# A fused adaLN transformer block, forward and backward: LN1, modulation and the first K, Q, V by chunks of 512 tokens between the first attention units, and db1 stored as a row

## The chip, the cores and the metric

The kernel runs on one core of one Trainium2 chip. The metric is the device time of one execution in microseconds (us), lower is better. Each result is the median of several executions on one chip, taken beside executions of the kernel before on the same chip.

## The reference

One block with 2048 tokens, width 512, 32 heads of 16, MLP width 1792, in bfloat16, and all its gradients from `grad_out`:

```python
mod = silu(c) @ w_mod                      # sa, ca, ga, sb, cb, gb: six rows of 512
h   = layernorm(x) * (1 + ca) + sa         # LN1 and modulation
x   = x + ga * (softmax_attention(h @ wqkv) @ wo)
h   = layernorm(x) * (1 + cb) + sb
x   = x + gb * (relu(h @ w1 + b1)**2 @ w2 + b2)
# outputs: x, dx, dwqkv, dwo, dw1, db1, dw2, db2, dc, dw_mod
```

## The kernel before

The forward attention runs over 64 units: four blocks of 512 queries, eight groups of four heads, two head pairs. Each unit has 16 steps of 128 keys: scores on TensorE, one exponential of 128x1024 on ScalarE, P·V on TensorE two steps later. "Background" generators give TensorE other work between the steps: in the first query block the K and Q of the other head groups, later the MLP. TensorE's order is the program's; the order on the other engines is a scheduler's.

Before the first unit the kernel does everything for LN1 at once (cuts marked `...`):

```python
# opening: modulation as full rows, then columns out of them
nc.sync.dma_start(wmod[:], io["w_mod"]...)                      # 3 MB
for (n0, nw) in chunks(6 * D, 512): ...                         # 24 matmuls 128x512
...
nc.scalar.activation(rstd[:], mv[:, :, 1], ACT.Sqrt, ...)       # LN1, all 16 token tiles
for st in range(ST):
    nc.scalar.activation(xhat_tm[:, st, :], x_tm[:, st, :], ACT.Identity, bias=nmr..., scale=rstd...)
...                                                             # all transposes, 1+ca into the weights
for t in range(2):
    for s0 in range(0, S, 512):
        for _ in self.gen_fm(ps, t, 0, s0, ...): pass           # K and Q of head group 0
...
load_q(0, 0, 0)                                                 # both back from DRAM
KT = load_k(0)
```

One block of K or Q, with its evicted copy (`ev_fm`) and its transposed copy for the backward pass (`ev_tm`):

```python
def gen_fm(self, ps, t, g, s0, eng="vector"):
    ...                                                          # 4 matmuls into PSUM
    nc.vector.tensor_scalar(ev[:], pt[:], bc, None, ALU.add)     # ev_fm
    nc.sync.dma_start((self.QTq_d, self.KTq_d)[t][g, :, s0:s0 + 512], ev[:])
    nc.sync.dma_start_transpose(tm[:]..., ev[:])                 # ev_tm
    nc.gpsimd.tensor_copy(tmc[:], tm[:, :, :, 0:DH])
    nc.gpsimd.dma_start((self.qtm_d, self.ktm_d)[t][g, ...], tmc[:]...)
```

At the end of each unit VectorE normalises the output:

```python
accbank = accp.tile([P, 2, 2, 4, DH + 1], F32, name="accbank")
...
acc = accbank[:, n % 2]
...
nc.vector.reciprocal(self.rl[...], acc[:, a, :, DH])
nc.vector.tensor_tensor(O32[...], acc[:, a, :, 0:DH], ..., ALU.mult)
```

At the transition from forward to backward:

```python
nc.gpsimd.memset(t[:], 0.0)                                      # eight masked K/V tiles, 128x2048
...
db1_b = w1p.tile([P, FT], BF16, name="db1_b", bufs=1)
nc.gpsimd.dma_start(io["out_5"].rearrange("(t p) -> p t", p=P), db1_b[:])   # db1 as a column
```

The softmax here doesn't subtract the row's maximum and nothing guards it: scores larger than these inputs give would overflow.

## Time and profile before

3033.77 us, median of three executions (3030.78 to 3035.01). The profiled one spans 3026.2 us. On the page, engines' busy time is given in tenths for 40 equal slices of some 76 us; this is ScalarE's row in the profile of before:

```profile
ACT  3489999999999974217777777777777777777443
```

A 9 means that ScalarE is busy for 90% or more of the slice, as in the forward attention; the first slices and slices 15 to 18 are where it starves. Counting exponentials in ScalarE's timeline gives stage borders, good to some 0.3 us:

| border, start in us | before |
|---|---|
| first exponential | 110.5 |
| first of the third unit (33rd) | 144.7 |
| first of the second query block (257th) | 369.4 |
| last of the forward pass | 1115.8 |
| first of the backward pass | 1348.2 |
| last of the backward pass | 2836.3 |
| span | 3026.2 |

A query block has 256 exponentials at a pitch of 0.925 us, which is 236.8 us; what it takes beyond that is stalls.

### The profile page before, as it was taken

What the parts mean: (1) busy time and instruction counts of PE and PEld (TensorE: products, weight loads), DVE (VectorE), ACT (ScalarE), POOL (GpSimd) and SP (SyncE); (2) the same over time, 40 slices, a digit from 0 to 9 for tenths busy, and PEclk for the clock granted to TensorE, in tenths of its full rate; (3) what the DMA queues carried; (4) which work ended last, traced back from release to release, by engine and by line L of the source; (5) the groups of instructions that cost most, each with busy time, mean ns of one, the idle gap of its engine ahead of it and who ended that gap; (6) DMA issues with size and microseconds to landing.
All of it is one profiled execution on the core that took longest, in us unless ns stands there. A gap on an engine that the chain in (4) does not pass through costs nothing. (4 is left out here: it accounts for less than half of the span.)

```text
span 3026.2 us, 72535 instructions
## 1 busy us (share of the span) xinstructions
PE 2726.1 (90%) x29894; PEld 1416.7 (47%) x30394; DVE 1797.7 (59%) x2804; ACT 2257.3 (75%) x3378; POOL 364.2 (12%) x616
## 2 busy tenths in 40 slices
PE   3689889999999997799999999999999999999796
PEld 1345545555555543644444444444444444444343
DVE  4422123322322343458878888888888888888575
ACT  3489999999999974217777777777777777777443
POOL 2343111320221132440000000000000000000000
PEclk7899999999999999899999999999999999999898
DMA  3974231530441347969999999999999999999941
GB/s 125 220 176 119 68 83 49 123 89 26 111 108 41 91 128 143 225 140 191 191 202 189 197 203 188 208 189 197 199 189 207 190 200 195 188 191 182 225 134 61
DMA packets 1305071, 467.71 MB, mean 155 GB/s; under 512 B 1237090, under 2 KB 1268836, under 8 KB 1304740
## 3 DMA queue, kind: packets, MB, share of 16 engines
q1 hardware_dynamic: 1275972, 376.78, 66.1%
q0 software_dynamic: 28240, 84.70, 10.1%
q8 instruction: 237, 3.88, 0.5%
q10 hardware_dynamic: 528, 1.57, 0.1%
q14 instruction: 94, 0.77, 0.1%
HBM read 85.99 MB, written 67.11 MB: 51 GB/s over the span
## 5 line engine op out<-in xcount | busy, mean ns | idle before, releaser
L1190 ACT ACTIVATE pu<-st 128x512 bf16<-128x512 f32 x2048 | 1133.3, 598 | 358.1 <-PE st L1188 302.3
L1195 DVE TENSOR_TENSOR ds<-dp,pu 128x1024 bf16<-128x1024 f32 x1024 | 1208.8, 1220 | 237.6 <-ACT pu L1190 229.7
L359 ACT ACTIVATE pu<-st 128x1024 bf16<-128x1024 f32 x1024 | 955.2, 1050 | 51.1 <-PE st L356 46.3
L1188 PE MATMUL st<-KTm,QTq 128*128 128x512 bf16 x2048 | 779.4, 381 | 12.2 <-ACT pu L1190 11.5
L1138 PEld LDWEIGHTS <-dsT 128*128 128x128 bf16 x8192 | 487.6, 96 | 493.9 <-DMA dsT<-ds 21.5
L1191 PE MATMUL dp<-VTm,dOTq 128*128 128x512 bf16 x1779 | 673.7, 379 | 7.2 <-DVE ds L1195 5.9
L356 PE MATMUL st<-QTm,KTq 128*128 128x512 bf16 x1937 | 591.1, 382 | 55.5 <-issue 17.6
L1138 PE MATMUL accq<-Kg,dsT 128*128 128x16 bf16 x8192 | 493.7, 170 | 30.8 <-DMA dsT<-ds 16.1
L326 PEld LDWEIGHTS <-pu 128*128 128x128 bf16 x8192 | 354.5, 96 | 297.0 <-issue 63.9
L326 PE MATMUL accbank<-Vaug,pu 128*128 128x17 bf16 x8192 | 358.5, 171 | 43.2 <-DVE O L334 35.0
L1118 PE MATMUL acckv<-ds,Qg 128*16 128x512 bf16 x2048 | 308.6, 381 | 0.9 <-DVE ds L1195 0.7
L1118 PE MATMUL acckv<-pu,dOg 128*16 128x512 bf16 x2048 | 308.6, 381 | 0.0
L1188 PEld LDWEIGHTS <-QTq 128*128 128x128 bf16 x2048 | 196.0, 96 | 219.6 <-issue 214.8
L356 PEld LDWEIGHTS <-KTq 128*128 128x128 bf16 x2048 | 194.2, 96 | 210.8 <-issue 164.6
L1191 PEld LDWEIGHTS <-dOTq 128*128 128x128 bf16 x2048 | 197.4, 96 | 37.9 <-DVE ds L1195 16.2
L1046 POOL DMA_DIRECT2D wqkv<-in_A_wqkv_dram x1 | 0.8, 791 | 1498.3 <-DMA dsT<-ds 1498.3
L462 DVE TENSOR_SCALAR ev_fm<-pps,bcol 128x512 bf16<-128x512 f32 x60 | 45.0, 751 | 145.4 <-PE pps L454 78.7
L333 DVE RECIPROCAL rl<-accbank 128x4 f32<-128x4 f32 x128 | 23.0, 180 | 179.0 <-PE accbank L326 178.9
L309 POOL DMA_DIRECT2D QTm<-QTq_d x128 | 65.1, 512 | 439.0 <-PE st L356 395.3
L916 DVE TENSOR_SCALAR rT<-pps,bias 128x512 bf16<-128x512 f32 x42 | 31.5, 751 | 116.1 <-PE pps L913 116.0
L924 DVE SCALAR_TENSOR_TENSOR auT<-pps,rT 128x512 bf16<-128x512 f32 x42 | 29.1, 692 | 86.1 <-PE pps L922 71.0
L454 PE MATMUL pps<-xhat1T,wpad 128*128 128x512 bf16 x223 | 78.5, 391 | 0.3 <-issue 0.2
(311 smaller groups left out, 2097.1 us busy)
## 6 DMA issues: line engine op xcount, KB each, us to landing
KTq<-KTq_d POOLq DMA_DIRECT2D x32, 512.0 KB, 3.8
duT_d<-auT POOLq DMA_DIRECT2D x4, 1792.0 KB, 8.2
aT_d<-rT POOLq DMA_DIRECT2D x4, 1792.0 KB, 12.8
QTq_d<-ev_fm SPq DMA_DIRECT2D x32, 128.0 KB, 2.4
QTm<-QTq_d POOLq DMA_DIRECT2D x128, 32.0 KB, 2.1
KTq_d<-ev_fm SPq DMA_DIRECT2D x32, 128.0 KB, 2.0
VTq_d<-vT POOLq DMA_DIRECT2D x4, 1024.0 KB, 6.2
O_d<-O POOLq DMA_DIRECT2D x4, 1024.0 KB, 6.2
```

What stands on the lines that cost most here:

```text
L309: nc.gpsimd.dma_start(QTm[j][32 * j:32 * j + 32, :], self.QTq_d[g, 32 * j:32 * j + 32, 512 * qc:512 * (qc + 1)])
L326: nc.tensor.matmul(acc[:, a, sub, :], lhsT=pu[:, a, sub * P:(sub + 1) * P], rhs=Vaug[:, kb, h, :], start=(kb == 0 and a == 0 and sub == 0) ...
L356: nc.tensor.matmul(stt[:, a, :], lhsT=KT[:, kb * P:(kb + 1) * P], rhs=QTm[2 * jp + a][:], start=True, stop=True)
L359: nc.scalar.activation(pu[:], stt[:], ACT.Exp, scale=self.scale)
L454: nc.tensor.matmul(pt[:], lhsT=self.wpads[t][:, kt, g, :], rhs=self.xhat1T[:, kt, s0:s0 + 512], start=(kt == 0), stop=(kt == DT - 1))
L462: nc.vector.tensor_scalar(ev[:], pt[:], bc, None, ALU.add)
L1118: nc.tensor.matmul(acckv[r:r + DH, :], lhsT=T[n][:, ib, col:col + DH], rhs=src[:, a, :], start=(ib == 0), stop=(ib == ST - 1))
L1138: nc.tensor.matmul(accq[:, ib, a, :], lhsT=dsT[:, (i * 2 + a) * 4 + sub, :], rhs=T["K"][:, 4 * c + sub, col:col + DH], start=(c == 0 and i ...
L1188: nc.tensor.matmul(stt[:], lhsT=T["QT"][:, q], rhs=masked["KT"][2 * jp + a][:, c0:c0 + 512], start=True, stop=True)
L1190: nc.scalar.activation(pu[:, a, :], stt[:], ACT.Exp, scale=self.scale)
L1191: nc.tensor.matmul(dp[:, a, :], lhsT=T["dOT"][:, q], rhs=masked["VT"][2 * jp + a][:, c0:c0 + 512], start=True, stop=True)
L1195: nc.vector.tensor_tensor(dsg[:, i], dp[:], pu[:], ALU.mult)
```

## The change

The intent: exponentials should start before LN1 is done for all tokens, and the K tile should not go through DRAM first. A generator does 512 tokens at a time: two chunks before the first scores, the third and fourth before key blocks 4 and 8 of the first unit. (1+ca) and sa are applied where the transposes are evicted, from modulation columns that come from one-column matmuls. Other parts: the masked memsets go to VectorE, db1 leaves as a row, O32 of the last block is loaded at once on SyncE, and the transposes of `wo` and `w2` come later.

```diff
-        load_q(0, 0, 0)
-        KT = load_k(0)
+        KT = kp.tile([P, S], BF16, name="KTq")
         with tc.manual_schedule(engines={mybir.EngineType.PE}):
+            first = self.gen_open(Vaug, KT, QTm, stp)
+            next(first)
 ...
                     if kb == ST // 2 and n + 1 < len(order):
+                        if n < 2 * NQ - 1 and jp == 1:
+                            bg.until(g + 1)
 ...
+                    if n == 0 and kb % 4 == 0:
+                        next(first, None)
 ... in gen_open, for each chunk of four token tiles:
+            nc.vector.tensor_scalar(ve[:, b], mv[:, b, 1], EPS, None, ALU.add)
+            nc.gpsimd.tensor_tensor(self.rstd1[:, b], ve[:, b], self.mhalf[:], ALU.pow)
+            nc.vector.scalar_tensor_tensor(nmr[:, b], ...)
 ...                                    xhat: odd tiles on GpSimd, even ones on ScalarE
+            tp = stp.tile([P, DT, 512], BF16, name="st")
+            for kt in range(DT):
+                for k in range(4):
+                    nc.tensor.transpose(tp[:, kt, k * P:(k + 1) * P], xhat1[...], self.ident[:])
+                if kt % 2:
+                    nc.vector.tensor_scalar(dst, tp[:, kt, :], self.opcaT[...], self.mod_col(0)[...], ...)
+                else:
+                    nc.scalar.activation(dst, tp[:, kt, :], ACT.Identity, bias=..., scale=...)
 ...                                    K of group 0 straight into KT, then V
-                nc.gpsimd.memset(t[:], 0.0)
+                nc.vector.memset(t[:], 0.0)
 ...
-            nc.gpsimd.dma_start(io["out_5"].rearrange("(t p) -> p t", p=P), db1_b[:])
+            nc.scalar.copy(db1_row[:, ft * P:(ft + 1) * P], csb_ps[0:1, :P])
+        nc.gpsimd.dma_start(io["out_5"].rearrange("(o f) -> o f", o=1), db1_row[:])
```

## The prediction

> **What bounds the kernel now.** One core, 3033.77 us. The page comes first: the forward attention holds ScalarE (1024 exponentials of 128x1024 in 955.2 us), the backward attention holds TensorE and VectorE, and its chain of waits covers only the last 10 us, so it says nothing about the rest. The row of 40 slices shows where no engine is full: the first slice, the second in part, and slices 15 to 18. I then read the busy time by stretches and got these stages: opening 0 to 110, attention over the first 512 queries 110 to 370, the other three query blocks to 1116, last MLP block and weight gradients 1116 to 1348, backward attention to about 2838, tail to 3027. The diff touches the first, the second and the fourth. So I asked each of those for its timeline and its waits.
>
> The opening: timeline of ScalarE from 0 to 200 us, then the waits of TensorE up to 110 us.
>
> ```profile
> 52.76 11.41 ACT L274 ACTIVATE xhat<-x,ln_nmr,rstd 128x512 bf16<-128x512 bf16 x16 [1.97 <-DVE ln_nmr L272]
> ...
> 109.16 1.28 ACT L359 ACT_TABLE_LOAD   x1 [25.57 <-PE st L356]
> 110.45 1.94 ACT L359 ACTIVATE pu<-st 128x1024 bf16<-128x1024 f32 x2
> ```
>
> ```profile
> PE st L356 <- issue: 17.4, 1, 17.4
> PE pps L415 <- DMA wqkv<-in_A_wqkv_dram: 17.0, 1, 17.0
> PE trps L252 <- ACT xhat L274: 15.5, 10, 11.9
> PE modps L205 <- DMA wmod<-in_w_mod_dram: 12.0, 1, 12.0
> ```
>
> The first exponential starts at 110.45 us. Four waits of TensorE sum to 61.9 us: it waits for the 3 MB modulation weights, then for weights and x, which are issued only at 26.8 us, then for LN1 on all 16 token tiles, and last for the K tile. The 17.4 us marked "issue" end at 108 us; the K tile's load was issued at 97.6 and its slowest landing is 11.7 us, so I read them as that round trip through DRAM, shared with a 1.8 MB weight load.
>
> The transition: waits of TensorE, then of GpSimd, from 1110 to 1365 us; the db1 store's own view; the GpSimd timeline.
>
> ```profile
> PE tp L574 <- DVE dOpad L1019: 19.1, 2, 16.2
> PE dps L760 <- DVE junk L769: 7.5, 1, 7.5
> PE dps L755 <- DVE junk L769: 6.9, 4, 2.5
> ```
>
> ```profile
> POOL out_dram L680 <- DMA out_dram<-db_b: 14.8, 1, 14.8
> ```
>
> ```profile
> DMA to landing us min/median/max: 24.5/24.5/24.5
> ```
>
> ```profile
> 1238.27 7.04 POOL L499 MEMSET KTm<- 128x2048 bf16 x4 [3.47 <-DMA dOTq_d<-dOTq]
> 1245.25 7.05 POOL L499 MEMSET VTm<- 128x2048 bf16 x4
> ```
>
> The column store of db1 takes 24.5 us to land. The next output store on GpSimd's queue stands 14.8 us behind it, the O32 load behind that store, VectorE behind the load, TensorE 16.2 us behind VectorE. A little later 14.1 us of memsets hold GpSimd's queue, so dW1 stores and w1 loads issue late, VectorE waits, and TensorE loses 7.5 us and part of the 6.9.
>
> **What the Trainium skill says.** (1) "DMA: Bandwidth & Descriptors", section "Rules for kernel authors": a strided, non-contiguous last dimension becomes one descriptor per element. Column db1 is 1792 elements of 2 bytes; the trace agrees: 24.5 us for 3.5 KB, and from 1204 to 1208 us the DMA share is 1.05 at only 24 GB/s. The column load of b1 landed in 3.3 us, so I expect nothing from replacing that. (2) "VectorE: DVE Perf Modes", section "Zero memsets can be issued as uint32 (trn2)": one cycle per element, and zeros of 2-byte elements may be written 4 bytes at a time. The built order of the changed kernel has its eight memsets as 128x1024. The trace of before has no such size; 128x128 took 165 ns and 128x512 485 ns, that is 0.83 ns per further element, so I estimate 0.91 us each, 7.3 us in all, against GpSimd's 14.1. (3) "TensorE: Matmul & The Clock Gate", section "What's actually happening": an idle array runs at half clock and warms only after some 3.4 us of work. The trace agrees: the granted clock is 0.50 from 1208 to 1216 us and 0.61 from 37 to 53 us, and matmuls of 128x512 there start 386 ns apart (12 in 4.63 us) against 215 when warm. So my opening has slow matmuls.
>
> **The change part by part.**
>
> *First exponential.* Loads of x, of two sixths of w_mod and of wqkv all go out in the first microseconds. They are 1 + 2 + 1.5 = 4.5 MB; before, 3 MB landed in 10.7 us, about 290 GB/s, so the last of them lands at about 17 us and the modulation columns at 9 to 10. The 32 one-column matmul pairs cost 0.10 us warm (0.096 us per weight load), twice that cold: done at about 15. The built order of VectorE puts all 16 bn_stats before the first chunk's "nmr", and two modulation copies that wait for those matmuls in the middle, so 15 + 11 x 0.58 + some 20 small operations, about 3 us, gives 25. ScalarE then makes two xhat tiles (0.7 each) while GpSimd has made its two. 16 cold transposes 2.5, evictions 1, four K matmuls, four Q and sixteen V at 0.25 to 0.38 each with their waits: 36 to 37. The order also puts chunk two whole (7 to 8 us) before the first scores: 44 to 45, first exponential about 46.5. Gain 110.45 - 46.5 = 64.
>
> *First unit.* Chunks three and four stand before key blocks 4 and 8. TensorE needs a score buffer, 16 transposes (1.7), evictions (1.5), 20 matmuls x 0.22 (4.4), less what overlaps: ScalarE sits idle about 6 us each, 12 us.
>
> *Rest of the first query block.* Before it took 369.6 - 110.45 = 259 us for 256 exponentials at 0.925 (96 of them in 88.81 us without a gap), which is 237: 22 us of stalls (6.8, 2.85, 1.84, 1.82 and small ones), partly from transposes of w2 that now move to later. In the changed order a new one appears: all 16 V transposes on SyncE and the four V stores on GpSimd come before the last K store and before the K load of the second head group. One V buffer makes a chain: four transposes, landing, store of 6.2 us, about 15 us per chunk and up to 20 where the 1.8 MB w1 load shares. Starting at 35.5 it ends at about 102, so K lands near 108, while the second group wants it at 46.5 + 32 x 0.925 + 12 = 88. If stores are faster, less: I take 18 us, plus 5 for small stalls. Sum of the two first stages: 64 + 22 - 12 - 18 - 5 = 51 us.
>
> *Transition.* The 16.2 us of TensorE's wait go: the row store is one small transfer at the end, and O32 is loaded whole on another queue. Of the 12 to 14 us around the memsets, half goes, because VectorE now has a 7.3 us burst. Together 22. Against that: three dU buffers instead of four, 1 MB more on SyncE before the dU transposes (4 us), 14 one-row ScalarE copies in slack; and the DMA engines are at 0.9 to 1.2 share from 1220 to 1280. The ten dU transposes (3.7 each) and the 24 us of backward loads that ran from 1225 to 1283 must still run; without the store they start about 15 us sooner. That is the limit: 14 us.
>
> *Elsewhere:* dW2 (3.7 us per a-block transpose against 3.55 of matmuls), backward attention and tail keep their length. Sum 51 + 14 = 65 us: 2968 to 2969.
>
> **The rivals.** *The V chain in front of K takes the gain.* For: the order above, and before the same kind of wait already cost 2.5 and 6.2 us. Against: each vT landed in 4.0 us median, so the chain may be shorter than I sum it. If it costs 35 instead of 18, the time is 2986. *The chain hides under other work:* then 15 us more is gained: 2953. *LN pieces on GpSimd or the clock become the bound of the opening:* GpSimd has 7.1 us of wpad memset, 2.3 of V ones, copies and a 1.05 us power before its first xhat, about 24 us by my count, one microsecond from the bound; first exponential at 55 gives 2977. *The transition is bound by DMA anyway*, and only 5 us of the 16 come through: 2978; or not at all bound, 34 us come through (TensorE's own 56 us of dW1 from 1198 on): 2949.
>
> **Range and chances.** Two per cent is 2973.1. My centre, 2968, is 5 us below. I allow about 15 us for the first two stages and 9 for the transition, 17 together, so 8 in 10 is 2944 to 2992. Faster by over 2%: 0.60; within: 0.39; slower: 0.01, since the 16.2 us of the store and most of 64 us at the front cannot both be lost.
>
> **What would show it.** First exponential at 44 to 50 us and two ScalarE gaps of 5 to 8 us in the first unit; a wait of scores for KTq of 10 to 25 us at the third unit; the first query block ending at 315 to 325. No wait behind the db1 store; dW2 starting about 14 us earlier relative to the end of the forward attention; VectorE memsets near 0.9 us. I am wrong if the first exponential is later than 55, if the third unit does not wait at all, or if the backward stage or the other query blocks change length by over 5 us.

## The result, and the profile after

The changed kernel takes 2997.52 us, median of four executions (2994.53 to 2998.36), against 3034.33 us for the kernel before in the same rounds: a ratio of 0.9879, 95% interval 0.9862 to 0.9896. Ratios are the mean time of one kernel's fast runs over that of the other's in the same rounds, so not quite the ratio of the medians. It is 1.2% faster, within 2%; I had predicted 2968 us, and 2997.5 lies outside my range of 2944 to 2992.

ScalarE's row after, to be held against that of before:

```profile
ACT  3599999999999974227777777777777777777443
```

Slices 2 and 3 are a little fuller, and the hole at slices 15 to 18 has hardly changed. By stages:

| border, start in us | before | after | gained in the stage | predicted |
|---|---|---|---|---|
| first exponential | 110.5 | 56.6 | 53.9 | 64 |
| 257th exponential | 369.4 | 352.5 | -37.0 | -13 |
| last of the forward pass | 1115.8 | 1099.9 | -1.0 | 0 |
| first of the backward pass | 1348.2 | 1320.4 | 11.9 | 14 |
| last of the backward pass | 2836.3 | 2804.4 | 4.1 | 0 |
| span | 3026.2 | 2995.3 | -1.0 | 0 |

The opening gains most of what was expected, but the first query block gives 37 us back. These are single profiles. Their scatter can be seen in two experiments below that leave the opening and the first block of before untouched: their first block took 263.8 and 263.7 us against 258.9 in the profile of before. So a stage difference of under 5 us means little.

The opening after: first ScalarE's timeline (start and duration in us, engine, line, operation, what it writes and reads, count, and in brackets the idle time before it and what ended it), then the waits of TensorE up to 57 us (total in us, times, longest).

```profile
32.90 1.52 ACT L396 ACTIVATE xhat<-x,nmr,rstd 128x512 bf16<-128x512 bf16 x2 [14.22 <-DVE nmr L390]
56.57 3.77 ACT L327 ACTIVATE pu<-st 128x1024 bf16<-128x1024 f32 x4 [6.85 <-PE st L324]
```

```profile
PE st L402 <- ACT xhat L396: 20.8, 2, 20.5
```

No trip of K through DRAM stands before the first exponential any more, and the only table load comes at 1.25 us. In their place TensorE waits 20.5 us for the first xhat, and ScalarE waited 14.22 us for `nmr`. VectorE's timeline tells why `nmr` is late; beside it stands GpSimd's.

```profile
13.49 9.07 DVE L388 TENSOR_SCALAR ve<-mv 128x4 f32<-128x4 f32 x1
...
32.71 0.15 DVE L390 SCALAR_TENSOR_TENSOR nmr<-mv,rstd 128x4 f32<-128x4 f32 x1
```

```profile
12.96 6.95 POOL L370 MEMSET wpad<- 128x4096 bf16 x2
19.86 2.25 POOL L375 MEMSET Vaug<- 128x512 bf16 x1
```

An operation of four elements per partition took 9.07 us. It began during the first of three GpSimd memsets and ended at 22.56, just after the third, which ends at 22.11. This looks like the rule on the Trainium skill's page "SBUF — State Buffer", section "SBUF: two separate sides": VectorE and GpSimd share one pair of ports as an exclusive lock; a VectorE operation in a mode that takes this second pair and a GpSimd operation exclude each other, and whoever comes second stands still. Experiment e1 tests it.

The first query block after, ScalarE's timeline (these are the three largest gaps):

```profile
70.27 3.77 ACT L327 ACTIVATE pu<-st 128x1024 bf16<-128x1024 f32 x4 [6.92 <-PE st L324]
83.94 10.58 ACT L327 ACTIVATE pu<-st 128x1024 bf16<-128x1024 f32 x11 [6.90 <-PE st L324]
131.82 1.02 ACT L327 ACTIVATE pu<-st 128x1024 bf16<-128x1024 f32 x1 [22.40 <-PE st L324]
```

The brackets of the first two show 6.9 us idle, but the exponentials stop for longer, since ScalarE evicts two transposes in between: from 60.34 (56.57 + 3.77) to 70.27 is 9.9 us, and again 9.9 before 83.94. TensorE's timeline shows the pace of a chunk, transposes waiting for each eviction in turn:

```profile
61.05 0.38 PE L402 MATMUL st<-ident,xhat 128*128 128x128 bf16 x4 [1.20 <-ACT xm1T L408]
62.15 0.38 PE L402 MATMUL st<-ident,xhat 128*128 128x128 bf16 x4 [0.71 <-DVE xm1T L405]
63.40 0.58 PE L402 MATMUL st<-ident,xhat 128*128 128x128 bf16 x4 [0.87 <-ACT xm1T L408]
```

The third gap is the one at the third unit. TensorE's waits from 57 to 353 us show what it waits for, and what else is left in this block. The wait that ended last is that for Q (`QTm`): the load of K was issued at 118.85 us, after the last V store at 116.70 on the same GpSimd queue, and landed at 126.8; that of Q was issued at 128.49 and landed at 130.4.

```profile
PE st L324 <- DMA QTm<-QTq_d: 17.0, 1, 17.0
PE accbank L289 <- DVE O L297: 9.1, 14, 4.2
PE pps L441 <- DVE ev_fm L450: 5.6, 2, 4.5
```

The transition after: waits of TensorE from 1090 to 1330 us; VectorE's first memset of the eight; the landing time of the db1 row.

```profile
PE dps L748 <- DMA du_blk<-duT_d: 6.9, 2, 5.6
PE pps L992 <- ACT dxT L569: 6.1, 1, 6.1
...
PE tp L568 <- DVE dOpad L1018: 2.5, 2, 1.3
```

```profile
1206.40 0.91 DVE L495 MEMSET KTm<- 128x1024 uint32 x1 [0.26 <-issue]
```

```profile
DMA to landing us min/median/max: 1.6/1.6/1.6
```

The wait of the transposes for dOpad is 1.3 us at most, where it was 16.2; nothing waits behind the db1 store; a memset takes the 0.91 us that I had estimated. In their place come 6.9 us of waits for dU transposes and 6.1 for the evicted transpose of dx1.

### The profile page after: what moved, and what is told of

It reads as the page before. It is cut to its first block, busy times and chain, and to the rows that moved or that the text cites. A ratio compares the mean times of both kernels' runs of the same rounds, so it can differ in the third digit from the quotient of the medians.

```text
span 2995.3 us, 72543 instructions
## 1 busy us (share of the span) xinstructions
PE 2714.6 (91%) x29931; PEld 1413.4 (47%) x30431; DVE 1799.5 (60%) x2728; ACT 2245.3 (75%) x3380; POOL 368.3 (12%) x617
## 5 line engine op out<-in xcount | busy, mean ns | idle before, releaser
L1187 PE MATMUL st<-KTm,QTq 128*128 128x512 bf16 x2048 | 779.0, 380 | 15.8 <-ACT pu L1189 11.6
L1137 PE MATMUL accq<-Kg,dsT 128*128 128x16 bf16 x8192 | 493.2, 170 | 30.2 <-DMA dsT<-ds 15.8
L1190 PEld LDWEIGHTS <-dOTq 128*128 128x128 bf16 x2048 | 197.4, 96 | 38.2 <-DVE ds L1194 16.2
L450 DVE CAST ev_fm<-pps 128x512 bf16<-128x512 f32 x60 | 41.5, 692 | 139.5 <-PE pps L441 90.1
L441 PE MATMUL pps<-xm1T,wpad 128*128 128x512 bf16 x217 | 78.2, 401 | 6.7 <-DVE ev_fm L450 5.6
```

The costliest lines, as they stand in the source:

```text
L441: nc.tensor.matmul(pt[:], lhsT=self.wpads[t][:, kt, g, :], rhs=self.xm1T[:, kt, s0:s0 + 512], start=(kt == 0), stop=(kt == DT - 1))
L450: nc.vector.tensor_copy(dst, pt[:])
L1137: nc.tensor.matmul(accq[:, ib, a, :], lhsT=dsT[:, (i * 2 + a) * 4 + sub, :], rhs=T["K"][:, 4 * c + sub, col:col + DH], start=(c == 0 and i ...
L1187: nc.tensor.matmul(stt[:], lhsT=T["QT"][:, q], rhs=masked["KT"][2 * jp + a][:, c0:c0 + 512], start=True, stop=True)
L1190: nc.tensor.matmul(dp[:, a, :], lhsT=T["dOT"][:, q], rhs=masked["VT"][2 * jp + a][:, c0:c0 + 512], start=True, stop=True)
```

## The experiments

All gave correct outputs. The column "against the change" is (ratio - 0.9879) times 3034.33 us. The intervals of the ratios are 0.15 to 0.4% to either side, that is 5 to 12 us, so the difference of two ratios is uncertain by some 7 to 9 us. The times of e1, e2b and e11 are at that limit or within it; what these runs show is in their gaps and borders. No run is called e8.

| run | edit | median us | ratio to before | against the change | first exp. | 33rd | 257th |
|---|---|---|---|---|---|---|---|
| change | | 2997.52 | 0.9879 | | 56.6 | 131.8 | 352.5 |
| e1 | GpSimd memsets earlier | 2992.22 | 0.9854 | -7.6 | 49.5 | 127.7 | 347.8 |
| e2 | V after K of groups 4 to 7 | 2990.63 | 0.9847 | -9.7 | 56.0 | 112.8 | 343.6 |
| e2b | V after all K | 2989.59 | 0.9854 | -7.6 | 57.0 | 112.9 | 345.9 |
| e3 | transposes in tiles apart | 2981.97 | 0.9827 | -15.8 | 49.7 | 119.1 | 338.7 |
| e4 | db1 as a column again | 3010.17 | 0.9921 | +12.7 | 56.0 | 132.3 | 352.5 |
| e5 | before + db1 row only | 3022.18 | 0.9960 | | 108.7 | 142.9 | 372.5 |
| e6 | before + VectorE memsets only | 3036.58 | 1.0011 | | 109.1 | 143.1 | 372.8 |
| e7 | e1 + e2b + e3 | 2969.98 | 0.9787 | -27.9 | 42.8 | 90.7 | 325.2 |
| e9 | e7 + six buffers | 2959.31 | 0.9759 | -36.4 | 42.9 | 90.8 | 323.2 |
| e10 | e7 + accumulators apart | 2942.93 | 0.9706 | -52.5 | 49.9 | 99.4 | 327.7 |
| e11 | change + six buffers | 2988.35 | 0.9858 | -6.4 | 58.3 | 132.1 | 351.7 |
| e12 | e9 + accumulators apart | 2935.54 | 0.9677 | -61.3 | 47.8 | 96.0 | 318.7 |
| e13 | before + accumulators apart | 3008.32 | 0.9910 | | 108.3 | 149.6 | 364.1 |
| e14 | change + accumulators apart | 2964.03 | 0.9752 | -38.5 | 57.7 | 129.4 | 340.6 |

### e1: is VectorE held up by GpSimd?

```diff
-        nc.gpsimd.tensor_scalar(t1[:], sig[:], -1.0, 1.0, ALU.mult, ALU.add)   # and three more, for dsilu
 ...
         for t in (1, 0):
             nc.gpsimd.memset(wpads[t][:], 0.0)
+        nc.gpsimd.memset(Vaug[:, :, :, DH:DH + 1], 1.0)
+        self.dsilu()                                    # the four operations, now behind the memsets
+        for t in (1, 0):
             for kt in range(DT):
```

> The changed kernel with one reorder: the four small GpSimd operations that wait for the sigmoid stand after the two wpad memsets and the V ones, so these 9 us of GpSimd work run before x lands instead of from 13.0 to 22.1 us. Theory (VectorE stands still behind GpSimd's instructions on a shared SBUF port): the four VectorE operations that took about 9 us at 13.5 take under 0.5 us, the first nmr comes at about 23 instead of 32.7, the first exponential at 46 to 49 instead of 56.6, and the time falls by 7 to 10 us, to about 2989. Rival (VectorE waited for the modulation columns or for x, and GpSimd was a bystander): those operations still end at about 22.5, first exponential 55 to 57, time 2995 to 2999.

GpSimd's three memsets in e1, then VectorE's timeline:

```profile
3.10 6.96 POOL L375 MEMSET wpad<- 128x4096 bf16 x2
10.00 2.25 POOL L376 MEMSET Vaug<- 128x512 bf16 x1
```

```profile
6.04 6.24 DVE L185 CAST cT<-cT_b 128x4 f32<-128x4 bf16 x1 [4.88 <-DMA cT_b<-in_c_dram]
...
15.48 0.16 DVE L395 TENSOR_SCALAR ve<-mv 128x4 f32<-128x4 f32 x1
...
25.09 0.14 DVE L397 SCALAR_TENSOR_TENSOR nmr<-mv,rstd 128x4 f32<-128x4 f32 x1
```

The stall moved with the memsets. The operation that took 9.07 us takes 0.16; now the first cast, which took 0.17 us, takes 6.24 and ends at 12.28, with the Vaug memset. That VectorE stands still while these memsets run is shown, and the bystander theory has fallen; that the reason is a pair of ports is what the page says. `nmr` comes 7.6 us earlier, the first exponential 7.1, both a little later than I expected, with a stall of 6.2 us still there; at the 33rd exponential 4.1 us of the gain remain. The skill's page lists copies, casts and tensor_scalar among the operations that can take the shared ports, and these are the ones that stood at the head of the stalls.

### e2 and e2b: is it V that stands in front of K?

```diff
+                ci = nc.gpsimd.tensor_copy(vp[:, :, 0:2, 0:DH], v[:, :, 2:4, :])
+                # first copy of each V chunk waits for the K eviction of group 4, 5, 6, 7 (e2b: 7, 7, 7, 7)
+                self.tc.add_manual_dep(ci.ins, last[(4, 5, 6, 7)[s0 // 4]].ins.name, SYNC_DEP, ...)
```

> The changed kernel with the 16 V transposes and four V stores made to wait for the K evictions of head groups 4 to 7. Theory of the prediction (the V chain stands in front of the second group's K on SyncE's and GpSimd's queues): ScalarE's gap at the third unit falls from 22.4 us to 5 to 9 (K of group 1 is still computed only from 94 us on, so some of the trip through DRAM stays), time down by 12 to 17 us, to about 2983. Rival (the gap is the late start of group 1 and its trip through DRAM, V is a bystander): gap 18 or more, time above 2993.

> The changed kernel with all 16 V transposes after the K evictions of the last head group. e2, where they stood among groups 4 to 7, took the third unit's gap from 22.4 to 5.3 us but got new gaps of 3.8 and 4.6 us there, and kept 7 us. Theory (V costs where K is made, as both use SyncE's transposes and GpSimd's queue): gap at the third unit again 5 to 6, no gap over 2 us at the later units, 13 to 17 us faster than the change, 2981 to 2985. Rival (V costs the same wherever it stands in the first query block): 2988 to 2992.

ScalarE's timeline in e2, then in e2b:

```profile
112.77 1.02 ACT L327 ACTIVATE pu<-st 128x1024 bf16<-128x1024 f32 x1 [5.34 <-PE st L324]
...
198.76 2.16 ACT L327 ACTIVATE pu<-st 128x1024 bf16<-128x1024 f32 x2 [3.75 <-PE st L324]
...
219.58 1.02 ACT L327 ACTIVATE pu<-st 128x1024 bf16<-128x1024 f32 x1 [4.60 <-PE st L324]
```

```profile
112.90 1.02 ACT L327 ACTIVATE pu<-st 128x1024 bf16<-128x1024 f32 x1 [4.36 <-PE st L324]
...
268.85 1.02 ACT L327 ACTIVATE pu<-st 128x1024 bf16<-128x1024 f32 x1 [10.16 <-PE st L324]
```

The gap at the third unit falls from 22.4 to 5.3 and 4.4 us: V was its cause, as predicted. But the time falls by only 8 to 10 us, because V makes a new stall where it goes: at 198.76 and 219.58 in e2, at 268.85 in e2b. At each of these places TensorE waits for VectorE's normalisation of the output (20.4 us of such waits in e2b's first 360 us, 9.6 the longest). In e2, between 190 and 225 us, VectorE itself waits 10.6 us for the buffers of transposed blocks, which stand behind V on SyncE's queue. So V costs less elsewhere, but not nothing, and my theory on e2b was wrong: its time is the rival's.

### e3: do the transposes wait for their own evictions?

```diff
-            tp = stp.tile([P, DT, 512], BF16, name="st")
             for kt in range(DT):
+                tp = ps.tile([P, 1024], BF16, name="pps")
```

> The changed kernel with each 128x512 transpose group in a PSUM buffer of its own (the three that the projections use) instead of slices of one tile shared with the scores. Theory (the one tile makes TensorE wait for each eviction before the next transposes, 2.5 to 3 us a chunk): the waits of the transposes for xm1T go from 0.7 to 1.2 us each to near zero, ScalarE's two gaps of 9.9 us become 7 to 8, first exponential at 51 to 53, time down by 7 to 10 us, to about 2989. Rival (the evictions themselves, 0.54 and 0.78 us in turn on two engines, set the pace, or the three buffers are too few): gaps shrink under 1 us, time 2994 to 2998.

ScalarE's timeline in e3:

```profile
49.66 3.77 ACT L327 ACTIVATE pu<-st 128x1024 bf16<-128x1024 f32 x4 [4.57 <-PE st L324]
59.38 3.77 ACT L327 ACTIVATE pu<-st 128x1024 bf16<-128x1024 f32 x4 [4.62 <-PE st L324]
```

From 53.43 to 59.38 is 5.95 us: this is the 6 us that I had predicted for the change. Each chunk is 4 us shorter, more than the 2.8 us of waits in the lines above. The rest is mostly the clock: the K and V matmuls behind the transposes take 5.8 us in the change (63.78 to 69.58), at a granted clock of 0.50 and then 0.85, and 4.55 us in e3 (54.14 to 58.69), at 1.00; in the next chunk the clocks are the same. The first exponential is 6.9 us earlier and the time 15.8 us shorter, about twice what I expected.

### e4, e5, e6: the transition taken apart

e4 is the changed kernel with the column store of the kernel before; e5 is the kernel before with only the row store; e6 is the kernel before with only this:

```diff
-                nc.gpsimd.memset(t[:], 0.0)
+                nc.vector.memset(t[:], 0.0)
```

> The changed kernel with db1 stored as a column again, as before (the rest of the change kept, O32 preloaded on SyncE). Theory (the cost of the column store was what stood behind it on GpSimd's queue, the O32 load above all, and that is now elsewhere): at most 5 us slower, 2997 to 3003. Rival (1792 descriptors of 2 bytes hold the DMA engines themselves): 8 to 16 us slower, 3006 to 3014.

> The kernel before with nothing but the row store of db1 in place of the column store. e4 lost 12.7 us when the column store came back. Theory (the column store alone is the transition's gain, because whatever stands behind it on GpSimd's queue waits for it): 10 to 14 us faster than before, 3020 to 3025, and the wait of the TensorE transposes for dOpad falls from 16.2 to under 4 us. Rival (the O32 load on SyncE and the memsets share the gain): 3 to 8 us faster, 3026 to 3032.

> The kernel before with nothing but the eight masked memsets moved from GpSimd to VectorE. The prediction gives half of the 12 to 14 us of waits around them: 4 to 7 us faster, 3027 to 3031. Rival (the DMA queue is full there and VectorE pays what GpSimd saves): within 2 us, 3032 to 3037.

GpSimd's waits from 1090 to 1345 us in e4:

```profile
POOL w_blk L788 <- DMA out_dram<-db_b: 9.8, 1, 9.8
```

The column costs 12.7 us although the O32 load no longer stands behind it: another load, of a w2 block, now stands there and waits 9.8 us, and the stores of `dOp_t` behind that. My theory, at most 5 us, was wrong; the rival, that the store holds the DMA engines themselves (8 to 16 us), has the time, and SyncE's queue bears it out. Its three transposes for dW2, in e4 and then in the change:

```profile
1186.39 25.54 SPq L786 DMA_TRANSPOSE a_blk<-aT_d  x3
```

```profile
1184.76 10.42 SPq L785 DMA_TRANSPOSE a_blk<-aT_d  x3
```

They are on another queue than the store and still take 15 us longer, and the next dU transpose starts at 1212.04 instead of 1195.28. From 1186 to 1198 us the DMA engines of e4 are busy at a share of 0.85 and move 38 GB/s; from 1185 to 1197 those of the change have 1.03 and 202 GB/s. So the store delays the transfers of both queues.

e5 agrees from the other side: the row alone gives 0.4%, 12 us by ratio (interval 4 to 21) and 7.0 by the borders of the stage (225.4 us against 232.4). TensorE's longest wait for dOpad is 3.0 us there, but its waits for `junk` grow from 14.4 to 20.1. e6 gives nothing (1.0011, interval 0.9982 to 1.0039). In its profile the dps waits for `junk` on VectorE go from 14.4 us to 10.1, but 5.4 us of waits for the masked K load appear, and the stage is 235.5 us long against 232.4. So the transition's gain is the store, or most of it: of 11.9 us, e4 loses 10.3 by the borders (230.8 against 220.5).

### e7: the three mends together

> The changed kernel with memsets early (e1), transposes in PSUM buffers apart (e3) and all V transposes after the last K (e2b). If the causes are separate, the gains add: first exponential at 42 to 43, ScalarE gaps in the first unit near 6 us, third unit's gap 5 to 8, time 2958 to 2966. Rival (the second head group's K, from the first bit of background work through the DRAM round trip, sets a floor that only moves the stall): third unit's gap 12 to 20 us, time 2970 to 2978.

The first exponential comes at 42.8 us, the two chunk gaps are 5.95 us, the third unit's is 4.5. These are the numbers of separate causes; yet the time, 2970, is at the edge of the rival's range. The times of e1, e3 and e2b add up to 31.0 us and e7 has 27.9, so within the noise they do add; I had expected more because I left out what e2b had lost. ScalarE's timeline shows these 10 us:

```profile
247.61 1.02 ACT L332 ACTIVATE pu<-st 128x1024 bf16<-128x1024 f32 x1 [10.47 <-PE st L329]
```

It is the stall that e2b has at 268.85.

### e9 to e12: the normalisation wait

```diff
 e9, e11:  self.open_pool("qkve", bufs=3, ...)  ->  bufs=6
 e10, e12, e13, e14:
-        accbank = accp.tile([P, 2, 2, 4, DH + 1], F32, name="accbank")
+        accbank = [accp.tile([P, 2, 4, DH + 1], F32, name=f"acc{i}") for i in range(2)]
-        self.mps = self.open_pool("mps", bufs=3, space=PSUM)
+        self.mps = self.open_pool("mps", bufs=2, space=PSUM)
```

> e7 (memsets early, transposes apart, V after all K) with six instead of three buffers for each evicted block and its transposed copies. e7 lost 10.5 us in one gap at 247.6 us, where TensorE waits 9.9 us for VectorE's normalisation of the output. Theory (that normalisation stands on VectorE's queue behind evictions that wait for a buffer, held by transposes queued behind V on SyncE): that gap falls under 3 us, time 8 to 12 us below e7, 2958 to 2962. Rival (SyncE's queue is simply full there, more buffers only fill later): gap over 7 us, 2966 to 2971.

> e7 with the output accumulators of successive units in two PSUM tiles of their own instead of two halves of one, paid for with two projection buffers instead of three. Theory (the first PV matmul of a unit waits for VectorE's normalisation of the unit before only because both lie in one tile): the waits for O, 20.9 us in the first 360 us and 20.2 us in the other query blocks, go below 3 each, also the 10.5 us gap, and the time falls by 15 to 30 us, to 2940 to 2955. Rival (two projection buffers slow the background work, or the scores set the pace at the boundary anyway): 2963 to 2975.

> The changed kernel with six instead of three of those buffers and nothing else. Theory (part of the third unit's 22.4 us gap is K evictions that wait for a buffer): TensorE's 5.6 us of waits for evictions go, the gap falls to 14 to 18, time 2989 to 2993. Rival (the V transposes and V stores ahead on the two queues set the gap whatever the buffers): gap 20 or more, 2995 to 2999.

> e9 and e10 together: six buffers and accumulators apart. If e10's theory holds, the buffers add little to it: 2938 to 2953, no gap of ScalarE over 3 us after the third unit in the first query block. If its rival holds, this is e9: 2958 to 2965.

The new tile needs a PSUM bank, so one projection buffer had to go; with all three kept it did not build. e9 comes out as its theory said in time, 8.5 us by the ratio below e7, about the size of the noise. The gap at 247.6 us is gone, but one of 5.8 us comes at 252.75, where TensorE waits for a load of Q. e11: the gap stays at 21.6 us, as the rival said; the 6.4 us of its time are within the noise, and no single stage of its profile explains them. In e10 all waits for O are gone from the list, in the first block and in the others; the last forward exponential starts 20.8 us earlier than in e7, though the first one comes 7.1 us later, with two projection buffers for transposes and projections. e12 combines both and is the fastest kernel: 2935.54 us, 3.2% below the kernel before. Gaps of 2.9 and 4.1 us are left in its first block after the third unit, where I expected none over 3.

### e13 and e14: whose stalls are these?

> The kernel before with the accumulators of successive units in two PSUM tiles and two projection buffers instead of three (the edit of e10 alone). The prediction put the 22 us of stalls of the first query block partly down to transposes of w2 and let all of them vanish with the change. Theory (most of them were waits of the PV matmuls for VectorE's normalisation, 12.9 us there, which the change leaves): the first query block shortens by 8 to 15 us from its 259, the other three together by 12 to 25, time 3000 to 3015. Rival (the stalls come from w2's transposes and the DMA queues, or two projection buffers cost as much): under 5 us in the first block, time 3018 to 3036.

> The changed kernel with the same edit alone. Theory: TensorE's waits for O (10.1 us in the first block, 22 in the other three) go below 2, the block after the third unit shortens by 5 to 10, the other three by 12 to 25, time 2970 to 2982; the third unit's gap stays at 18 to 24. Rival (transposes and V projections then fight for two buffers, or the gaps at the unit boundaries come from the scores): 2988 to 3000.

From the third unit to the end of the first block lie 224 exponentials, 207.2 us of pitch. The kernel before takes 224.7 us there (369.4 - 144.7), e13 takes 214.5; the change takes 220.7, e14 takes 211.2. So of 17.5 us of stalls before, some 10 went with the shared tile (15 against e5 and e6, which take 229.6 and 229.7 us there), and of 13.5 after, 9.5. In query blocks two to four e13 gains 21.7 us (746.4 to 724.7) and e14 21.3. For e13's first block as a whole the theory said 8 to 15 and it is 3.1 against the profile of before (8 against those of e5 and e6), because a new wait of 10.6 us for the K tile comes at the third unit. e14 gains more than I expected, 38.5 us by ratio and 30.5 by its profile; its third gap is 12.4 us after another of 6.8. By ratio the same edit gives 27 us in e13, 24.6 in e10 (against e7) and 24.9 in e12 (against e9), so its worth is 25 to 38 us. Tiles apart also lie in other places of PSUM; whether the tile or the place ties the units is not separated.

## Why the prediction was wrong

The prediction's sum was 51 us for the first two stages and 14 for the transition. Term by term, from the two profiles:

| term | predicted | measured |
|---|---|---|
| first exponential earlier | 64 | 53.9 |
| two gaps in the first unit | -12 | -19.8 |
| stall at the third unit | -18 | -22.4 |
| old stalls gone, less small new ones | 22 - 5 = 17 | 22.1 - 16.9 = 5.2 |
| first two stages | 51 | 16.9 |
| transition | 14 | 11.9 |

The fourth row comes from the first query block as a whole: 22.1 us of stalls before (258.9 - 236.8), 59.1 after (295.9 - 236.8), of which the three gaps are 42.2 and other stalls 16.9 (that the fifth row has the same number is chance). The first two stages miss by 34.1 us, and no single term carries it.

**The first exponential, 10.1 us short.** The step that failed is "gives 25" for the chain on VectorE: `nmr` came at 32.7, because the sum had durations of VectorE's operations but not that GpSimd's memsets could hold them. I had counted those same memsets, among the rivals, only as GpSimd's own time. In e1, where they lie earlier, `nmr` comes at 25.09, and the first exponential 7.1 us sooner. Also "evictions 1" for four evictions was too little: they alternate with the transposes through one PSUM tile, and e3 takes 6.9 us off the two chunks. Together they give 42.8 us (e7), less than my 46.5, so other terms of that sum were too high by some 4 us.

**The gaps in the first unit, 7.8 us short.** I wrote that TensorE's parts come to about 6 us "less what overlaps". Next to nothing overlaps while one tile is transposed into and evicted from in turn: transposes and evictions take 4.3 us (59.47 to 63.78) where I had 1.7 + 1.5, and the 20 matmuls 5.8 where I had 4.4 at the full clock. With tiles apart the gap is 5.95 us: the size was right for a kernel that the diff does not contain. The order of instructions that I read does not show this wait; the tile's allocation line in the diff does.

**The third unit, 4.4 us short.** The mechanism was right: the V chain stands in front of the second group's K, and the gap was predicted as 18. e2 and e2b show that V is 17 to 18 of the 22.4 us. What the sum left out is the load of Q behind that of K: it landed 3.6 us later (130.4 against 126.8), and it is the wait that TensorE's list names, not KTq as I had said. That the difference came out so near is partly luck: K landed at 126.8 us and not at 108, and the second group wanted it at some 106 (56.6 + 32 x 0.925 + 19.8) and not at 88.

**The old stalls, 11.8 us short, the largest term.** The sum has "+ 22": all of those stalls were to vanish, as they came "partly from transposes of w2 that now move to later". The step that failed is that they all vanish. For the largest one the cause was right; SyncE's and VectorE's timelines of before:

```profile
138.60 10.51 SPq L859 DMA_TRANSPOSE W2gbT<-w  x1
```

```profile
152.72 0.75 DVE L462 TENSOR_SCALAR ev_fm<-pps,bcol 128x512 bf16<-128x512 f32 x1 [5.82 <-DMA ev_tm<-ev_fm]
```

The transposed block that VectorE waits for stands behind w2's transpose on SyncE's queue, the normalisation of the output behind that eviction, and TensorE waits 6.2 us; the prediction took these 6.2 us for a wait of the V chain's kind. In the change w2 stands at the end of the same block, and the scaling of w2, 8.5 us of VectorE in a row, stands in front of another normalisation. VectorE's and ScalarE's timelines after:

```profile
329.64 8.52 DVE L855 TENSOR_TENSOR w<-w,mod 128x512 bf16<-128x512 bf16 x14 [9.52 <-DMA w<-in_B_w_dram]
```

```profile
340.24 45.29 ACT L327 ACTIVATE pu<-st 128x1024 bf16<-128x1024 f32 x48 [4.37 <-PE st L324]
```

This is read from the traces; no run moves w2 alone. The waits of TensorE for `O`, 12.9 us in that block in the profile of before, were in the profile, and I did not ask for each of them whether the change takes it away. This is their line, from the waits of TensorE in the profile of before from 110 to 370 us:

```profile
PE accbank L326 <- DVE O L334: 12.9, 15, 6.2
```

After the change 9.1 us of them are left. They come from two units' accumulators in one tile and from what stands before the normalisation on VectorE's queue; e13 and e14 show that about 10 us of stalls go with the tile in both kernels.

**The transition.** 11.9 us for a predicted 14, and the limit was about right. Its parts were not, so the sum was partly lucky: the row store gives all or most of it (12 us by ratio and 7.0 by the borders in e5, 12.7 and 10.3 in e4), and the half of the memset waits that was to go gives nothing that can be measured (e6). The path was not only GpSimd's queue either: the column held SyncE's transposes as well (e4).

**The signs.** Of those that I had named, the memsets (0.91 us), the missing wait behind the db1 store and dW2 (its first matmul 11.8 us earlier after the last forward exponential) came true; the first exponential (56.6), the two gaps (9.9) and the end of the first query block (352.5, not 315 to 325) did not.

**Elsewhere.** Query blocks two to four and the tail kept their length to 1.0 us. The backward attention is 4.1 us shorter, which I do not explain: over all the profiles that stage varies from 1481 to 1489 us.

The range was too narrow. It took the errors of the parts for independent, and the 0.60 for "faster by over 2%" follows from it and from a centre 5 us below that border. They were not independent: each of the four terms of the first stages left out a wait that the change adds or keeps, so all missed on the same side. One rival named the first of them in effect ("LN pieces on GpSimd ... first exponential at 55 gives 2977") and was close in place, 56.6 us, though for another reason.

## What to carry to other kernels

When work is moved to start earlier, ask for each new short operation which engine runs beside it on a shared port, and put the long fills of the other engine where both are idle; here a pure reorder of four small operations moved the first exponential by 7 us. A tile that one engine fills by slices while another drains it makes the two take turns, and two accumulators in one tile tie a unit to the end of the one before: tiles apart were worth 16 us for the transposes and 25 to 38 us for the accumulators here, the latter about as much as the whole change (37 us). And before letting an old stall "vanish", name what each of its waits is for, and check that the change touches that.

## What the Trainium skill lacked or had wrong

- "SBUF — State Buffer", "SBUF: two separate sides", says that the shared ports are held for the whole instruction and that the other engine blocks. Here the wait went on over several instructions: a VectorE operation of 128x4 waited 9.07 us through three GpSimd memsets in a row (6.95 us for two, then 2.25), and in e1 one waited 6.24 us until the last of them ended. The page does not say who gets the ports between two instructions of a run. It is not always GpSimd: in the changed kernel a VectorE operation that began at 28.69 ended at 31.34, between two GpSimd memsets that run from 30.36 to 32.21.
- "DMA: Bandwidth & Descriptors", "Rules for kernel authors", gives the one descriptor per element, and the landing time of 24.5 us agrees with it. It has no figure for what that does to other transfers: the next one on GpSimd's queue waited 14.8 us in the kernel before and 9.8 us in e4, three transposes on SyncE's queue took 25.54 us in e4 against 10.42, and e4 is 12.7 us slower than the change.
- No page that I read has a price for neighbours in one PSUM tile that two engines use in turn: 15.8 us for the transposes (e3) and 24.6 to 38.5 us for the accumulators (e10, e12, e13, e14).
